# The prologue of a fused attention and SiLU kernel: key loads by slot, another order of value and query loads, the last exponentials ahead of the first product

## The chip, the cores and the metric

The kernel runs on one core of a Trainium2 chip. The time is device microseconds of one execution; the kernel before was run five times, with a median of 285.71 us (284.96 to 286.09). One more execution was taken with the hardware profiler, and all durations inside the kernel come from that one. Its own time was 285.76 us, of which 283.8 us lie between its first and its last instruction.

## The reference

Eight batches of eight heads, 576 positions and head dimension 64 go through attention over pooled keys and values: groups of eight neighbouring positions of k and v are averaged to 72, so that each head has 576 queries and 72 keys. The result, 4608 tokens of 512 features, goes through a two-layer network with SiLU.

```python
k_p = k.reshape(B, H, Sp, pool, D).mean(axis=3)          # Sp = 72, pool = 8, D = 64
v_p = v.reshape(B, H, Sp, pool, D).mean(axis=3)
scores = scale * np.matmul(q, k_p.transpose(0, 1, 3, 2))
attn = np.exp(scores - np.max(scores, axis=-1, keepdims=True))
attn = attn / (np.sum(attn, axis=-1, keepdims=True) + 1e-09)
x = np.matmul(attn, v_p)                                  # then (tokens, 512)
h = x @ w_in                                              # 512 x 2048
g = h * (1.0 / (1.0 + np.exp(-h)))
out = g @ w_out                                           # 2048 x 512
```

## The kernel before

The tokens are worked in nine stages of 512 columns (NT = 9, NTT = 512). In each stage the up-product `up` multiplies the attention result xT with w_in, 128 hidden rows at a time, ScalarE applies SiLU and writes h_T, and then the down-product multiplies with w_out and stores. Attention for the next batch is laced into the products of the stage as fillers: `spread` runs a filler after a given step (a step is one matmul of a product). The order of instructions on each engine is the order in which the program writes them; nothing reorders them (`manual_schedule`). Each engine works through its own queue in that order and waits where an operand is not ready.

PSUM has two kinds of bank: three are called "mm" and five "at". A tile asked for under a name takes a bank of that kind that must have been read by its last reader; a matmul into it waits for that reader.

Before stage 0 there is a prologue, and it alone is touched by the change. It makes attention of the first query group of batch 0, so that the first product can begin. Its pieces:

- Keys and values of batch 0 lie as 576 rows (head and pooled position) of 8 x 64 float32, cut in slots of 128 rows: four full slots and a rest of 64 rows (`load_slots`, L245). Slots 0 to 2 are in one tile, slots 3 and 4 in another. Key slots go over the queues of SP and ScalarE; values, queries and weights go over POOL's queue, which converts queries and weights to bf16 on the way.
- `slot_sums` (L263) adds the eight positions in VectorE: 512 to 256 to 128 to 64 columns a slot, for all slots of a tile in one instruction per halving.
- `select_k` (L283) sorts the summed rows by head with small matmuls against an identity matrix that POOL makes (memset and mask, L714 and L715); a copy puts the result in SBUF. `select_v` (L299) does the same for values with a shifted identity.
- `q_transpose` (L150) transposes 32 x 32 blocks of one head half and one query half on VectorE.
- `scores` (L337) makes four PSUM tiles ("at" banks) and four exponentials on ScalarE; `denominators` (L357) sums them with matmuls and takes the reciprocal with a logarithm and an exponential on ScalarE (in stage 0, for the two late parts, with a reciprocal on VectorE, 1.9 us each); `numerators` (L376) multiplies exponentials and values, and VectorE multiplies with the reciprocal into xT.
- A part is one half of the heads (the first number) and one half of the queries (the second). Parts (0, 0) and (1, 0) give the first 288 columns of xT, with which the first product starts; parts (0, 1) and (1, 1) give the next 288, and their denominators and numerators are fillers of the first up-product, at steps 1, 5, 13 and 17.
- `warm_up` (L696) are matmuls of zeros that keep TensorE busy between the pieces.

The first up-product runs 128 hidden rows (a group g, four steps) over 288 columns for g = 0 to 10, then over the remaining 224, then g = 11 to 15 over all 512. Each group writes one "mm" bank, so that the fourth group waits for the first group's SiLU. ScalarE must load another function table (L408, `moe_tables`) between the last exponential and the first SiLU.

On POOL each load waits for the landing of the load eight places before it, because eight semaphores go round. The functions that the change touches and what calls them:

Of the kernel before, what the change touches and what calls it, by code (L numbers as in the profile page):

```python
# [27 lines left out]
FP32 = mybir.dt.float32  # L28
# [8 lines left out]
def kernel(  # L37
# [9 lines left out]
    nc = tc.nc  # L47
# [6 lines left out]
    d_ff = moe_w_in.shape[1]  # L54
# [36 lines left out]
    def ps_tile(shape, dtype, tag, name):  # L91
        return psum.tile(shape, dtype, tag=tag, bufs=banks[tag], name=name)
# [4 lines left out]
    ident = shifts[:, SP : SP + 128]  # L97
    ones = singles.tile([SP, 32], BF16, name="ones")
    warm = singles.tile([128, 512], BF16, name="warm")
    w_in_sb = singles.tile([128, KF, d_ff], BF16, name="w_in_sb")  # L100
    w_out_sb = singles.tile([128, KG, d_model], BF16, name="w_out_sb")
    w_sum = singles.tile([128, 5, KQ, CQ], BF16, name="w_sum")
# [21 lines left out]
    def load_q_half(b, f):  # L124
        for a in range(2):
            es = slice(f * QF * D, (f + 1) * QF * D)
            nc.gpsimd.dma_start(out=batches[b]["q_bf"][:, a, es], in_=q_r[b][:, a, es])
# [22 lines left out]
    def q_transpose(b, a, f):  # L150
        st = batches[b]
        n = QF * D
        nc.vector.transpose(  # L153
            out=st["qT"][:, a, f * QF : (f + 1) * QF].rearrange("r i c p -> r (i c p)"),
            in_=st["q_bf"][:, a, f * n : (f + 1) * n],
        )
# [88 lines left out]
    def load_slots(eng, b, name, i0, i1, half=None):  # L245
        es = slice(0, RE) if half is None else slice(half * RE // 2, (half + 1) * RE // 2)
        src = (k if name == "k" else v)[b].rearrange("h (sp p) d -> (h sp) (p d)", p=POOL)
        src = src[:, es]
        how = dict(accum_op=ALU.add) if half else {}
        tiles = row_tiles[name]  # L250
        w = es.stop - es.start
        if i0 == SLOTS:
            eng.dma_start(
                out=tiles[1][:REST, SLOTS - SA, :w], in_=src[128 * SLOTS :], **how
            )
        else:
            j = i0 // SA
            eng.dma_start(
                out=tiles[j][:, i0 - SA * j : i1 - SA * j, :w],
                in_=src[128 * i0 : 128 * i1].rearrange("(i r) e -> r i e", r=128), **how  # L260
            )

    def slot_sums(name, j, halves=False):  # L263
        raw = row_tiles[name][j]
        dst = rows5[name][:, SA:] if j else rows5[name][:, :SA]
        w = RE // 4 if halves else RE // 2
        while w > D:
            nc.vector.tensor_add(  # L268
                out=raw[..., :w], in0=raw[..., :w], in1=raw[..., w : 2 * w]
            )  # L270
            w //= 2
        nc.vector.tensor_add(out=dst, in0=raw[..., :D], in1=raw[..., D : 2 * D])
# [26 lines left out]
    def select_v(b, a, tag="at"):  # L299
        st = batches[b]  # L300
        if a == 0:
            st["v_ps"] = ps_tile([128, H, D], FP32, tag, "v_ps")
            st["vp"] = mid.tile([SP, H, D], BF16, tag="vp", name="vp")
        for h in range(4 * a, 4 * (a + 1)):
            segs = list(segments(h))
            for j, (i, r, sp, m) in enumerate(segs):
                x = SP + r - sp
                nc.tensor.matmul(
                    st["v_ps"][:, h, :], lhsT=shifts[:, x : x + 128], rhs=v5[:, i],
                    start=(j == 0), stop=(j == len(segs) - 1),  # L310
                )
# [7 lines left out]
    def part(g, f):  # L319
        return ((g, f * QF, (f + 1) * QF),)  # L320
# [16 lines left out]
    def scores(b, segs):  # L337
        st = batches[b]
        w = width(segs)
        sc = [ps_tile([128, 512], FP32, "at", "sc_ps")[:SP, :w] for s in range(4)]  # L340
        for g, i0, i1, cs in seg_cols(segs):
            for c in range(2):
                for s in range(4):
                    rows = slice(32 * s, 32 * (s + 1))
                    nc.tensor.matmul(  # L345
                        sc[s][:, cs],
                        lhsT=kz[b % 2][rows, g, c, :],
                        rhs=st["qT"][rows, g, i0:i1, c, :],
                        start=(c == 0), stop=(c == 1),
                    )  # L350
        es = mid.tile([SP, 4, VW], BF16, tag="es", bufs=4, name="es")[:, :, :w]
        for s in range(4):
            nc.scalar.activation(es[:, s, :], sc[s], func=AF.Exp, scale=score_scale)  # L353
        st["es", segs] = es


    def denominators(b, segs, on_dve=False):  # L357
        st = batches[b]
        w = width(segs)
        es = st["es", segs]  # L360
        den_ps = ps_tile([128, 512], FP32, "at", "den_ps")
        for s in range(4):
            nc.tensor.matmul(  # L363
                den_ps[32 * s : 32 * (s + 1), :w],
                lhsT=ones, rhs=es[:, s, :], start=True, stop=True,
            )
        rec = mid.tile([128, VW], FP32, tag="rec", bufs=4, name="rec")[:, :w]
        if on_dve:
            nc.vector.reciprocal(rec, den_ps[:, :w])
        else:  # L370
            lnd = mid.tile([128, VW], FP32, tag="lnd", name="lnd")[:, :w]
            nc.scalar.activation(lnd, den_ps[:, :w], func=AF.Ln)  # L372
            nc.scalar.activation(rec, lnd, func=AF.Exp, scale=-1.0)
        st["rec", segs] = rec
# [29 lines left out]
    def attn_tables():  # L404
        nc.scalar.preload_act_table_set("natural_log_exp_and_others")
# [124 lines left out]
            pass  # L530

    def plain(t, step, g, n0, n):
        hp_ps = ps_tile([128, 512], FP32, "mm", "hp_ps")
        c0 = (t * NTT + n0) % NX

        for r0, r1 in ((0, min(n, NX - c0)), (min(n, NX - c0), n)):
            for kk in range(KF) if r1 > r0 else ():
                if r0 == 0:
                    next(step)
                x0 = (c0 + r0) % NX  # L540
                nc.tensor.matmul(  # L541
                    hp_ps[:, r0:r1],
                    lhsT=w_in_sb[:, kk, g * 128 : (g + 1) * 128],
                    rhs=xT[:, kk, x0 : x0 + r1 - r0],
                    start=(kk == 0), stop=(kk == KF - 1),
                )
        nc.scalar.activation(h_T[:, g, n0 : n0 + n], hp_ps[:, :n], func=AF.Silu)  # L547
# [148 lines left out]
    def warm_up(n):  # L696
        for _ in range(n):
            nc.tensor.matmul(warm_ps, lhsT=warm[:, :128], rhs=warm, start=True, stop=True)  # L698

    load_slots(nc.sync, 0, "k", 0, 2)  # L700
    load_slots(nc.scalar, 0, "k", 2, 3)
    load_slots(nc.scalar, 0, "k", 3, 4)
    load_slots(nc.sync, 0, "k", 4, 5)
    load_q(0, halves=True)
    load_q_half(0, 0)
    load_slots(nc.gpsimd, 0, "v", 0, 3)
    load_q_half(0, 1)
    load_slots(nc.gpsimd, 0, "v", 3, 4)
    load_slots(nc.gpsimd, 0, "v", 4, 5)
    attn_tables()  # L710
    nc.vector.memset(warm, 0.0)
    nc.vector.memset(ones, float(POOL))
    nc.vector.memset(kp, 0.0)
    nc.gpsimd.memset(shifts, 0.0)  # L714
    make_identity(nc, ident, nomemset=True)  # L715

    for n in "kv":
        nc.vector.memset(row_tiles[n][1][REST:, SLOTS - SA], 0.0)
# [1 line left out]
    def load_w_in(c0, c1):  # L720
        for g in range(2):
            nc.gpsimd.dma_start(
                out=w_in_sb[:, 2 * g : 2 * g + 2, c0:c1], in_=w_in_r[g][:, :, c0:c1]
            )
# [6 lines left out]
        load_w_in(512 * c, 512 * (c + 1))  # L731

    act_copy = nc.scalar.copy
    warm_up(19)
    slot_sums("k", 0)
    select_k(0, 0)
    copy_k(0, 0, act_copy)
    warm_up(4)
    q_transpose(0, 0, 0)
    scores(0, part(0, 0))  # L740
    slot_sums("k", 1)
# [3 lines left out]
    q_transpose(0, 1, 0)  # L745
    warm_up(2)
    scores(0, part(1, 0))
    denominators(0, part(0, 0))
    slot_sums("v", 0)
    warm_up(2)  # L750
    select_v(0, 0, "mm")
    copy_v(0, 0, act_copy)
    denominators(0, part(1, 0))
    q_transpose(0, 0, 1)
    scores(0, part(0, 1))
    slot_sums("v", 1)
    warm_up(1)
    numerators(0, part(0, 0), ("mm", "at"))
    warm_up(2)
    select_v(0, 1, "mm")  # L760
    copy_v(0, 1)
    q_transpose(0, 1, 1)
    warm_up(2)
    numerators(0, part(1, 0), ("mm", "at"))
    scores(0, part(1, 1))
    warm_up(2)
    load_slots(nc.gpsimd, 1, "k", 0, 3)
    load_slots(nc.gpsimd, 1, "k", 3, 4)
    load_slots(nc.gpsimd, 1, "k", 4, 5)
    load_q(1)  # L770
    load_w_in(1536, d_ff)
    for c in range(3):
        load_w_out(c)
    load_slots(nc.gpsimd, 1, "v", 0, 3)
# [142 lines left out]
```

The softmax here doesn't subtract the row's maximum and nothing guards it: scores larger than these inputs give would overflow.

## Time and profile before

| | |
|---|---|
| median of five runs | 285.71 us (284.96 to 286.09) |
| profiled execution, its own time | 285.76 us |
| its span, first to last instruction | 283.8 us |
| TensorE busy (matmul) | 276.4 us, 97% of the span |
| VectorE busy | 225.6 us, 79% |
| ScalarE busy | 183.8 us, 65% |
| POOL busy | 60.7 us, 21% |
| first matmul of the first up-product | 17.48 us after the start of the span |
| from then without a gap of TensorE | from 21.93 us, to 28.00 us and on |

Times inside the profile are microseconds from the first instruction. A line of a timeline gives start, length, engine, source line, operation, written and read tiles with shapes, how many instructions were merged in it, and in brackets how long the engine stood idle before it and what ended the wait. The matmul lengths contain the fill of the array, so that back-to-back matmuls start closer together than they are long. A line of the list of DMA issues gives the tiles, the queue, how many issues, their size (in the type of the destination) and the time from issue to landing.

### The profile page before, as it was taken

Reading aid. Unit: us, or ns where it says so; the run is one execution under the profiler, and the core shown is the slowest. Engines: PE = TensorE matmul, PEld = TensorE weight load, DVE = VectorE, ACT = ScalarE, POOL = GpSimd, SP = SyncE. Lnnn points to the kernel's source line nnn. Section 1 sums busy time; section 2 is a strip of 40 time slices with the busy share of each in tenths; the row PEclk is TensorE's granted clock in tenths of the full one; section 3 lists DMA queues with packets and bytes.
Section 4 is the critical chain, followed back from the end, with each engine's and each line's share of the span. In section 5 each row is a group of like instructions: output and inputs, shape, how many; then the busy total and the mean of one; then the engine's idle time right before and its main releaser. Section 6 shows DMA issues by size and latency. Waiting matters only on the chain.

```text
span 283.8 us, 6889 instructions
## 1 busy us (share of the span) xinstructions
PE 276.4 (97%) x2773; PEld 194.6 (69%) x2793; DVE 225.6 (79%) x404; ACT 183.8 (65%) x359; POOL 60.7 (21%) x78
## 2 busy tenths in 40 slices
PE   8989999999999999999999999999999999999995
PEld 3338544466777677767888786688667767787684
DVE  4887836989978898879896998799888786836773
ACT  1678676568567875687668857885779467326700
POOL 8654316342140214021402130542000000000000
PEclk9999999999999999999999999999999999999999
DMA  7999998895749763985498539597830032005003
GB/s 205 280 259 229 211 308 170 235 180 102 152 59 198 171 132 49 190 202 108 77 195 178 88 85 178 131 141 112 144 91 0 2 98 52 2 17 132 1 18 133
DMA packets 31376, 37.70 MB, mean 133 GB/s; under 512 B 10352, under 2 KB 22256, under 8 KB 31344
## 3 DMA queue, kind: packets, MB, share of 16 engines
q0 software_dynamic: 23840, 26.77, 52.1%
q1 hardware_dynamic: 6928, 9.58, 12.2%
q10 hardware_dynamic: 576, 0.92, 0.9%
q8 instruction: 22, 0.36, 0.5%
q14 instruction: 10, 0.08, 0.1%
HBM read 36.70 MB, written 9.44 MB: 163 GB/s over the span
## 4 chain that ended last, share of the span: by engine, by line
PE 93%; DVE 3%; ACT 2%; issue 1%; DVEq 0%
PE hp_ps L541 25%; PE o_psP L649 15%; PE o_psQ L649 15%; PE u_psP L482 7%; PE u_psQ L482 7%; PE o_psR L649 5%; PE sc_ps L345 4%; PE o_ps L576 3%; PE warm_ps L698 3%; PE nu_ps L389 2%; PE u_psR L482 2%; PE den_ps L363 2%; ACT es L353 1%; DVE w_sum L627 1%; DVE xT L398 1%
## 5 line engine op out<-in xcount | busy, mean ns | idle before, releaser
L541 PE MATMUL hp_ps<-xT,w_in_sb 128*128 128x512 bf16 (+3 forms) x397 | 80.1, 338 | 1.4 <-ACT h_T L547 0.4
L649 PEld LDWEIGHTS <-h_sum 128*128 128x128 bf16 x640 | 60.6, 98 | 11.9 <-issue 1.3
L547 ACT ACTIVATE h_T<-hp_ps 128x512 bf16<-128x512 f32 (+2 forms) x95 | 51.4, 546 | 25.2 <-PE hp_ps L541 24.2
L541 PEld LDWEIGHTS <-w_in_sb 128*128 128x128 bf16 x412 | 39.3, 98 | 25.0 <-issue 1.4
L609 DVE TENSOR_TENSOR h_sum<-h_T 128x1024 bf16<-128x1024 bf16 (+1 forms) x72 | 50.9, 744 | 7.0 <-ACT h_T L547 7.0
L353 ACT ACTIVATE es<-sc_ps 72x384 bf16<-72x384 f32 (+1 forms) x100 | 39.1, 470 | 10.0 <-PE sc_ps L345 10.0
L482 PEld LDWEIGHTS <-w_sum 128*128 128x128 bf16 x300 | 29.4, 98 | 7.7
L649 PEld LDWEIGHTS <-h_T 128*128 128x128 bf16 x256 | 24.1, 98 | 4.4 <-issue 0.9
L398 DVE TENSOR_TENSOR xT<-nu_ps,rec 128x384 bf16<-128x384 f32 (+1 forms) x50 | 23.9, 532 | 0.2
L372 ACT ACTIVATE lnd<-den_ps 128x384 f32<-128x384 f32 (+1 forms) x23 | 11.2, 485 | 19.3 <-PE den_ps L363 19.3
L153 DVE STREAM_TRANSPOSE qT<-q_bf 128x576 bf16<-128x576 bf16 x32 | 23.0, 755 | 0.4 <-DMA q_bf<-in_q_dram 0.4
L490 ACT ACTIVATE h_T<-c_sb 128x512 bf16<-128x512 f32 x30 | 18.1, 627 | 5.7 <-DVE c_sb L514 5.7
L268 DVE TENSOR_TENSOR raw<-raw 128x384 f32<-128x384 f32 (+3 forms) x20 | 12.3, 617 | 8.0 <-DMA raw<-in_v_dram 5.0
L177 POOL DMA_DIRECT2D raw<-in_k_dram x5 | 7.2, 1430 | 52.8 <-DMA raw<-in_k_dram 52.8
L553 POOL DMA_DIRECT2D out_dram<-o_sb x1 | 0.6, 617 | 79.7 <-issue 79.7
L649 PE MATMUL o_psP<-w_out_sb,h_sum 128*128 128x256 bf16 x128 | 17.6, 273 | 0.0
L514 DVE TENSOR_TENSOR c_sb<-u_psP,t_sb 128x512 f32<-128x512 f32 x15 | 10.3, 689 | 8.2 <-PE u_psP L482 3.6
L649 PE MATMUL o_psQ<-w_sum,h_sum 128*128 128x256 bf16 x128 | 16.7, 273 | 0.0
L649 PE MATMUL o_psQ<-w_out_sb,h_sum 128*128 128x256 bf16 x128 | 16.6, 273 | 0.0
L649 PE MATMUL o_psP<-w_sum,h_T 128*128 128x256 bf16 x128 | 16.5, 273 | 0.0
L649 PE MATMUL o_psQ<-w_sum,h_T 128*128 128x256 bf16 x128 | 16.5, 273 | 0.0
L649 PE MATMUL o_psR<-w_sum,h_sum 128*128 128x256 bf16 x128 | 15.7, 273 | 0.0
(80 smaller groups left out, 439.3 us busy)
## 6 DMA issues: line engine op xcount, KB each, us to landing
out_dram<-o_sb SPq DMA_DIRECT2D x128, 64.0 KB, 4.5
raw<-in_k_dram POOLq DMA_DIRECT2D x10, 576.0 KB, 10.0
raw<-in_v_dram POOLq DMA_DIRECT2D x10, 576.0 KB, 8.0
q_bf<-in_q_dram POOLq DMA_DIRECT2D x6, 576.0 KB, 13.6
w_in_sb<-in_moe_w_in_dram POOLq DMA_DIRECT2D x8, 256.0 KB, 8.4
w_out_sb<-in_moe_w_out_dram POOLq DMA_DIRECT2D x4, 512.0 KB, 13.9
raw<-in_v_dram POOLq DMA_DIRECT2D x2, 768.0 KB, 11.4
raw<-in_k_dram POOLq DMA_DIRECT2D x1, 768.0 KB, 10.1
```

The costliest lines, as they stand in the source:

```text
L153: nc.vector.transpose(out=st["qT"][:, a, f * QF : (f + 1) * QF].rearrange("r i c p -> r (i c p)"), in_=st["q_bf"][:, a, f * n : (f + 1) * n],)
L268: nc.vector.tensor_add(out=raw[..., :w], in0=raw[..., :w], in1=raw[..., w : 2 * w])
L345: nc.tensor.matmul(sc[s][:, cs], lhsT=kz[b % 2][rows, g, c, :], rhs=st["qT"][rows, g, i0:i1, c, :], start=(c == 0), stop=(c == 1),)
L353: nc.scalar.activation(es[:, s, :], sc[s], func=AF.Exp, scale=score_scale)
L372: nc.scalar.activation(lnd, den_ps[:, :w], func=AF.Ln)
L398: nc.vector.tensor_mul(out=xT[:, 2 * g0 + c : 2 * (g0 + ng - 1) + c + 1 : 2, cols], in0=nu[c][:, :w].rearrange("r (g n) -> r g n", g=ng), ...
L482: nc.tensor.matmul(ps[bank][:, u, :], lhsT=w[:, kk, 128 * u : 128 * (u + 1)], rhs=x[:, kk, :], start=first and u == 0 and kk == 0, stop=kk ...
L490: nc.scalar.activation(h_T[:, g : g + 2, j * NQ : (j + 1) * NQ], src, func=AF.Silu)
L541: nc.tensor.matmul(hp_ps[:, r0:r1], lhsT=w_in_sb[:, kk, g * 128 : (g + 1) * 128], rhs=xT[:, kk, x0 : x0 + r1 - r0], start=(kk == 0), stop= ...
L547: nc.scalar.activation(h_T[:, g, n0 : n0 + n], hp_ps[:, :n], func=AF.Silu)
L609: nc.vector.tensor_tensor(out=h_sum[n][:, ks, :], in0=quarter(*a, ks), in1=quarter(*b, ks), op=op)
L649: nc.tensor.matmul(ps[b][:, c, :], lhsT=left(n, kt, c), rhs=W_OUT[n][:, kt, :], start=b not in begun, stop=kt == k1 - 1, skip_group_check= ...
```

## The change

Everything but `slot_sums` (which can now work on some of a tile's slots) and one bank in `plain` is the order of the prologue:

- Key slots are loaded one by one, in turn over SP (slots 0, 2, 4) and ScalarE (slots 1, 3). Before, SP took slots 0 and 1 in one load and then slot 4, ScalarE slots 2 and 3.
- Slot 0 is summed alone, then slots 1 and 2.
- The 19 warm-up matmuls before the first selection become eight, and eight float32 matmuls of 128 columns that read key slots 0 and 2, four each, and so wait for these loads (`warm_behind`). A float32 tile of zeros is their other operand. Other warm-ups are fewer or placed anew.
- On POOL's queue the identity's memset and mask go ahead of the values, and all values ahead of the second query half.
- On VectorE the sums of the last two value slots go ahead of the second query half's transposes, and both transposes ahead of the first multiplications into xT. The second copy of values moves from VectorE to ScalarE.
- The scores of the second query half go behind the second selection of values; so their exponentials stand together at the end of the prologue on ScalarE.
- The fourth group of the first product takes an "at" bank instead of an "mm" bank.
- Of the later loads, the last quarter of w_in goes ahead of the next batch's queries.

```diff
-    def slot_sums(name, j, halves=False):
-        raw = row_tiles[name][j]
-        dst = rows5[name][:, SA:] if j else rows5[name][:, :SA]
+    def slot_sums(name, j, halves=False, part=slice(None)):
+        raw = row_tiles[name][j][:, part]
+        dst = (rows5[name][:, SA:] if j else rows5[name][:, :SA])[:, part]
...
     def plain(t, step, g, n0, n):
-        hp_ps = ps_tile([128, 512], FP32, "mm", "hp_ps")
+        tag = "at" if (t, g, n0) == (0, 3, 0) else "mm"
+        hp_ps = ps_tile([128, 512], FP32, tag, "hp_ps")
...
-    load_slots(nc.sync, 0, "k", 0, 2)
-    load_slots(nc.scalar, 0, "k", 2, 3)
-    load_slots(nc.scalar, 0, "k", 3, 4)
-    load_slots(nc.sync, 0, "k", 4, 5)
+    def warm_behind(rhs, n):
+        for _ in range(n):
+            nc.tensor.matmul(
+                warm_ps[:, : rhs.shape[-1]], lhsT=warm32, rhs=rhs, start=True, stop=True
+            )
+
+    for i in range(SLOTS + 1):
+        load_slots((nc.sync, nc.scalar)[i % 2], 0, "k", i, i + 1)
     load_q(0, halves=True)
     load_q_half(0, 0)
+    nc.gpsimd.memset(shifts, 0.0)
+    make_identity(nc, ident, nomemset=True)
     load_slots(nc.gpsimd, 0, "v", 0, 3)
-    load_q_half(0, 1)
     load_slots(nc.gpsimd, 0, "v", 3, 4)
     load_slots(nc.gpsimd, 0, "v", 4, 5)
+    load_q_half(0, 1)
     attn_tables()
     nc.vector.memset(warm, 0.0)
+    nc.vector.memset(warm32, 0.0)
...
-    nc.gpsimd.memset(shifts, 0.0)
-    make_identity(nc, ident, nomemset=True)
...
-    warm_up(19)
-    slot_sums("k", 0)
+    warm_up(8)
+    warm_behind(row_tiles["k"][0][:, 0, RE - 128 :], 4)
+    warm_behind(row_tiles["k"][0][:, SA - 1, RE - 128 :], 4)
+    slot_sums("k", 0, part=slice(0, 1))
+    slot_sums("k", 0, part=slice(1, SA))
     select_k(0, 0)
     copy_k(0, 0, act_copy)
-    warm_up(4)
+    warm_up(2)
...
+    slot_sums("v", 0)
+    warm_up(1)
     denominators(0, part(0, 0))
-    slot_sums("v", 0)
-    warm_up(2)
+    warm_up(3)
     select_v(0, 0, "mm")
     copy_v(0, 0, act_copy)
     denominators(0, part(1, 0))
+    slot_sums("v", 1)
     q_transpose(0, 0, 1)
-    scores(0, part(0, 1))
-    slot_sums("v", 1)
-    warm_up(1)
-    numerators(0, part(0, 0), ("mm", "at"))
-    warm_up(2)
-    select_v(0, 1, "mm")
-    copy_v(0, 1)
     q_transpose(0, 1, 1)
     warm_up(2)
+    numerators(0, part(0, 0), ("mm", "at"))
+    warm_up(1)
+    select_v(0, 1, "mm")
+    copy_v(0, 1, act_copy)
+    warm_up(2)
+    scores(0, part(0, 1))
     numerators(0, part(1, 0), ("mm", "at"))
+    warm_up(1)
     scores(0, part(1, 1))
-    warm_up(2)
...
+    load_w_in(1536, d_ff)
     load_q(1)
-    load_w_in(1536, d_ff)
```

More of the change, by code (lines that the diff above doesn't have):

```diff
@@ L99 @@
     warm = singles.tile([128, 512], BF16, name="warm")
+    warm32 = singles.tile([128, 128], FP32, name="warm32")
     w_in_sb = singles.tile([128, KF, d_ff], BF16, name="w_in_sb")
```

## The prediction, made before the changed kernel was run

> **What bounds the kernel now.** I read the page first, for where TensorE isn't full:
>
> ```profile
> span 283.8 us, 6889 instructions
> PE 276.4 (97%) x2773; PEld 194.6 (69%) x2793; DVE 225.6 (79%) x404; ACT 183.8 (65%) x359; POOL 60.7 (21%) x78
> PE   8989999999999999999999999999999999999995
> ```
>
> TensorE is at 9 everywhere but in the first three slices (7.1 us each) and the last. A change to the prologue is worth what it moves the moment from which TensorE streams the first product without a hole. The chain that ended last, in order of time (start, length, what), says when that is:
>
> ```profile
> 1.20 6.68 PE warm_ps L698 x19
> ...
> 16.67 0.48 PE sc_ps L345 x8
> 17.15 1.29 ACT es L353 x4
> ...
> 18.45 1.28 ACT L408
> ...
> 19.75 0.42 ACT h_T L547
> ...
> 20.21 0.41 PE hp_ps L541 x2
> 20.62 0.36 PE nu_ps L389 x8
> 20.98 0.59 PE hp_ps L541 x4
> 21.57 0.36 PE nu_ps L389 x8
> 21.93 6.07 PE hp_ps L541 x55
> ```
>
> The end is set by ScalarE: last exponentials to 18.44, table load, first silu at 19.75, and only its result frees a PSUM bank. Up to there TensorE's work is filler or waits. From 21.93 it streams (up to 28.00 without a gap), so my yardstick is this point: 18 steps of the first product done, both late numerators done. VectorE's timeline (start, length, [idle before]) shows what feeds the start:
>
> ```profile
> 5.32 1.55 DVE L268 TENSOR_TENSOR raw<-raw 128x768 f32<-128x768 f32 x2 [2.69 <-DMA raw<-in_k_dram]
> 7.66 0.78 DVE L153 STREAM_TRANSPOSE qT<-q_bf 128x576 bf16<-128x576 bf16 x1 [0.40 <-DMA q_bf<-in_q_dram]
> 8.36 1.11 DVE L268 TENSOR_TENSOR raw<-raw 128x512 f32<-128x512 f32 x2
> 10.41 1.51 DVE L268 TENSOR_TENSOR raw<-raw 128x768 f32<-128x768 f32 x2
> 13.39 1.15 DVE L268 TENSOR_TENSOR raw<-raw 128x512 f32<-128x512 f32 x2 [0.40 <-DMA raw<-in_v_dram]
> ```
>
> It waits for keys to 5.32, for queries to 7.66, and is then almost without a hole to 13. The DMA issues, asked one by one, give landings (last number, us from issue):
>
> ```profile
> q_bf<-in_q_dram POOLq DMA_DIRECT2D x1, 144.0 KB, 6.4
> raw<-in_k_dram SPq DMA_DIRECT2D x1, 512.0 KB, 4.5
> ```
>
> So the first query part, issued at 1.27, lands at 7.67, and slots 0 and 1 (issued 0.74) at 5.24.
>
> **The change, part by part.**
>
> *Keys by slot.* SP carries the same bytes in the same order (slots 0, 2, 4 for 0-1, 4), ScalarE likewise (1, 3 for 2, 3); one more issue on SP (0.44 us) has nothing behind it before the stores. So slot 0 lands earlier and slot 2 at about 5.24. Slot 0's sums (rows 128x256 0.42, 128x128 0.29, plus a smaller one) lie beside the loads. Slot 0 is done when slot 2 lands, so only two slots are left to sum: the row for two slots runs from 8.36 to 9.80, 1.44, against 1.95 for three (5.32 to 7.27). First keys at 6.76: 0.51 earlier.
>
> *Fillers ahead of them.* Warm-ups stand 0.43 apart before 6 us (12 in 5.17) and 0.22 after; the 19 hold TensorE to 7.81. Eight now end at 4.6. Eight float32 matmuls of 128 columns follow, which no row shows. Floor: small selection matmuls, 12 in 0.22, so 0.02 each; ceiling: three 128x512 warm-ups each. I take one 128x512, the row nearest in place, bank and bytes: 3.5 of them at 0.43 to 6.1, 4.5 at 0.22, end 7.1. Selection of keys then starts at 7.1, not 7.81, and the keys (6.76) don't hold it. [...]
>
> *First scores.* The copy of the keys would end at 7.7, but the query part still lands at 7.67: it stays first on POOL's queue. Its transpose ends at 8.44, scores start at 8.47 (8.99 before: two fillers fewer). [...] The trace's 6.4 decides: keys half a microsecond earlier buy nothing by themselves.
>
> *VectorE to 12.31* keeps its rows: keys 8.36 to 9.80, transpose to 10.48, values 10.41 to 12.31. On ScalarE the exponentials start at 8.94 and 10.98 (9.46 and 11.44): 0.46 earlier.
>
> *POOL's order.* The memset (0.43) and mask (0.52) now go before the first value load, which is issued at 3.5, not 2.48. It landed at 2.48 + 7.6 = 10.1 with the queue busy with queries till then; cost on landing between 0 and 1.0. I take 0, since the queue is behind and VectorE needs it at 10.41. The mask is ready at 3.5, long before 7.1. The other values (landed 4.33 + 8.4 = 12.7 and 13.3) change places with the second query half (10.6 and 11.3): 384 KB of values overtake 288 KB of queries read, and landed 2.0 behind the last of these (13.3 - 11.3), so they come at most 2.0 behind the first values: 12.1; the queries then close the group at 13.3. VectorE's hole of 0.40 at 13.39 goes: values 12.23 to 13.67, both transposes to 15.05, four products to 16.6. Later loads keep their bytes ahead.
>
> *TensorE and ScalarE, 12.36 to 18.3.* Value selection 12.36 to 12.63, denominators to 12.9, two fillers to 13.3; the value copy on ScalarE ends at 13.31; numerators 13.37 to 13.9; filler, second selection 14.1 to 14.5; its copy, now on ScalarE, 14.55 to 14.9; two fillers; scores of the second query half at 14.87, where before it was 13.05. Their exponentials start at 15.34 (before 14.47), so this step is 0.87 late. The last scores reuse those four banks: the fourth waits for the fourth exponential, 16.62, then 0.05 + 0.29 (one matmul) + 0.04 puts the last exponentials at 17.0 to 18.3 (before 17.14 to 18.44). Table load to 19.59, first silu at 19.6: 0.15 gained, no more.
>
> *The extra bank.* The fourth column group now writes an "at" bank, so TensorE no longer waits at 20.21: groups 0 to 3 and the first numerators are done at 20.2 (last exponentials 18.3, denominators to 18.6, 10 steps of 0.12, numerators 0.36). But the second numerators' second half then takes the bank of group 3 and waits for its silu: three pitches of (1.02 - 0.41)/2 = 0.30 after 19.6, plus 0.41, so 20.95; half of 0.36 follows, and the yardstick is passed at 21.2 instead of 21.86 to 21.93: 0.65 gained (0.15 ScalarE, 0.5 bank).
>
> *Behind it.* The next batch's queries go behind the last up-weights: they landed at 15.41 + 11.9 = 27.3, the weights at 29.9; swapped, queries at 29.9, so the transposes (29.57) start 0.3 later and end at 32.65; scores read them at 34.76 - 0.65. Weights come earlier than needed. The first down-weights landed at 19.78 + 12.7 = 32.5, used at 34.24; 1.1 is left. The next keys' sums end at 26.7 (landing 13.27 + 10.1), selection at 27.93 - 0.65. All cover holds for a gain up to about 1.1.
>
> Sum: 285.76 (profiled run; span 283.8 and 1.96 around it) - 0.65 = 285.1. The median of the runs, 285.71, is 0.05 lower than the profiled one, so 285.1 stands for it too.
>
> **Rivals.**
>
> *The fillers become the bound (slower).* If a float32 matmul costs two or three 128x512 pieces instead of one, TensorE is late for the selection of the keys, and the scores, exponentials and copies behind it are late with it. For it: no float32 matmul is in the trace, and each of the eight brings its weights again. [...] With two (0.86, after 6.1 0.43) the eight end at 8.8, scores start at 9.45, and each step to the silu is 0.93 later: 286.0. With three, 10.2 and 287.4. Up to 7.8 they cost nothing; it turns a loss from selection at 8.5, and one over 0.2% from about 9.0, 2.1 pieces.
>
> *Nothing moves.* The late second-half scores eat the bank's gain: a slip of 0.5 between 12.36 and 14.87 (the value loads landing at 11.0, or the copy on ScalarE behind a late denominator) goes straight through the 15.34: 285.6. For it: six operations of three engines stand in a row there. Against: 0.3 to 0.4 of slack at each load.
>
> *Queries earlier too.* With the values a microsecond behind, the first queries could land at 7.1; the two fillers and the copy then bind (7.85), everything to 12.36 moves 0.6: 284.5. Against: the queries are ahead of the values in one queue already.
>
> **How the numbers follow.** Forecast 0.50 (284.8 to 285.5), nothing moves 0.20 (285.4 to 286.0), fillers 0.18 (286.0 to 287.4), earlier queries 0.12 (284.4 to 284.8). 0.2% is 0.57 us, about what these runs can tell: faster is below 285.14, slower above 286.28. Of the forecast 0.40 is below, 0.10 within; with the queries, faster 0.52. Same: 0.10 + 0.18 + 0.03 = 0.31; slower 0.15 + 0.02 = 0.17. The range 284.4 to 286.3 leaves out the dear end of the fillers.
>
> **What would show it.** First selection at 7.1 and scores at 8.5; VectorE's query wait still ending near 7.66 and no wait at 13.4; last exponentials at 17.0 just behind the ones before; silu at 19.6; no wait of the product for a silu, but one of about 0.5 of the second numerators; the product's unbroken stretch from 21.2. Wrong if float32 matmuls hold TensorE past 8, if the first value sums start after 10.6, or if the span behind 21 us changes length.

## The result and the profile after

The changed kernel takes 285.83 us (median of 44 runs, 284.88 to 289.14); the kernel before, timed beside it, 285.35 us (78 runs, 284.88 to 286.13). The ratio is 1.0025, 95% interval 1.0015 to 1.0034: slower, by little more than the 0.2% that such a measurement can tell. The forecast was 285.1, or 0.998 as a ratio to the five runs' median of 285.71 that it started from. The profiled execution of after took 287.06 us, with a span of 284.7 us.

The median doesn't tell all. The span is listed for each run: the median span of after is 284.05, against 283.5 for 35 runs of before, and 9 of the 44 runs have a mean granted TensorE clock of 0.981 to 0.994 and spans of 284.6 to 287.4. No run of those 35 is under 0.997 or above 284.1. Most of the loss isn't in the nine: the 35 runs of after at 0.997 or more have a median of 285.77 us.

The page of after, the lines that answer to those shown of before:

```profile
span 284.7 us, 6902 instructions
PE 275.7 (97%) x2777; PEld 196.1 (69%) x2797; DVE 226.1 (79%) x407; ACT 184.5 (65%) x360; POOL 60.6 (21%) x78
PE   8799998999999999999999999999999999999995
```

Two slices lost their 9: the second, 7.1 to 14.2 us, where the prologue has a hole that it hadn't before, and the seventh, 42.7 to 49.8. TensorE's timeline of after (start, length, [idle before]) shows both holes:

```profile
4.59 2.74 PE L704 MATMUL warm_ps<-raw,warm 128*128 128x128 f32 x16
7.25 0.28 PE L291 MATMUL kz_ps<-shifts,k 128*32 128x72 bf16 x12
8.00 0.44 PE L346 MATMUL sc_ps<-qT,kz 32*72 32x288 bf16 x8
...
13.65 0.34 PE L309 MATMUL v_ps<-v,shifts 128*128 128x64 bf16 x6 [1.82 <-DVE v L273]
...
15.98 0.44 PE L346 MATMUL sc_ps<-qT,kz 32*72 32x288 bf16 x8
...
21.75 0.69 PE L390 MATMUL nu_ps<-es,vp 72*32 72x288 bf16 x8
22.37 6.14 PE L543 MATMUL hp_ps<-xT,w_in_sb 128*128 128x288 bf16 x55
...
43.89 1.03 PE L578 MATMUL o_ps<-w_out_sb,h_T 128*128 128x512 bf16 x4 [0.16 <-issue]
45.44 0.59 PE L578 MATMUL o_ps<-w_out_sb,h_T 128*128 128x512 bf16 x2 [0.52 <-DMA w_out_sb<-in_moe_w_out_dram]
```

Up to 10 us all is near the forecast (keys selected at 7.25 for 7.1) or earlier (first scores at 8.00 for 8.47). Then the selection of the values stands at 13.65 behind 1.82 us of idle TensorE. The unbroken stretch of the first product starts at 22.37, against 21.86 before and 21.2 forecast. And at 45.44, in the first down-product, TensorE waits for down-weights; before had no such wait. The rows of before for the selection, the unbroken stretch and POOL's first value load:

```profile
12.36 0.33 PE L308 MATMUL v_ps<-v,shifts 128*128 128x64 bf16 x6 [0.17 <-DVE v L272]
...
21.86 6.14 PE L541 MATMUL hp_ps<-xT,w_in_sb 128*128 128x288 bf16 x55
...
2.48 0.79 POOL L258 DMA_DIRECT2D raw<-in_v_dram  x1
```

What the first hole waited for, in VectorE's and POOL's timelines of after:

```profile
7.13 0.78 DVE L154 STREAM_TRANSPOSE qT<-q_bf 128x576 bf16<-128x576 bf16 x1 [0.24 <-DMA q_bf<-in_q_dram]
11.65 1.55 DVE L269 TENSOR_TENSOR raw<-raw 128x768 f32<-128x768 f32 x2 [1.70 <-DMA raw<-in_v_dram]
```

```profile
2.48 0.42 POOL L712 MEMSET shifts<- 128x328 bf16 x1
2.97 0.29 POOL masks.py:199 TENSOR_SCALAR_AFFINE_SELECT shifts<-shifts 128x128 bf16<-128x128 bf16 x1
3.21 1.34 POOL L259 DMA_DIRECT2D raw<-in_v_dram  x2
```

The first value load, now behind memset and mask, is issued 0.73 later than before (2.48) and its sums start 1.24 later (10.41). The load lands in sixteen parts, each with a time of its own in the trace, and the sums wait for the last. In before the parts land between 9.59 and 10.04; in after the first at 9.17 and the eighth and ninth about 9.59, earlier than before, but the last five at 10.68 to 11.63. From there ScalarE's chain keeps its forecast lengths, only late (its timeline of after):

```profile
18.14 1.30 ACT L354 ACTIVATE es<-sc_ps 72x288 bf16<-72x288 f32 x4 [0.40 <-PE sc_ps L346]
19.46 1.28 ACT L409 ACT_TABLE_LOAD   x1
20.76 1.32 ACT L549 ACTIVATE h_T<-hp_ps 128x288 bf16<-128x288 f32 x4
```

The chain of waits of after between 27 and 46 us has for the second hole:

```profile
27.89 17.51 DMA w_out_sb<-in_moe_w_out_dram
45.40 0.04 issue
45.44 0.59 PE o_ps L578 x2
```

This is the last quarter of the down-weights. Before, it was no matter; in the timeline of before and in the answer on this tile (fewest, median and most us from issue to landing) stand:

```profile
43.38 1.46 PE L576 MATMUL o_ps<-w_out_sb,h_T 128*128 128x512 bf16 x6 [0.16 <-issue]
...
L728 POOL DMA_DIRECT2D w_out_sb<-in_moe_w_out_dram x4: 742/751/770, 19.8 to 28.9; - x4
DMA to landing us min/median/max: 12.7/13.9/14.8
```

The last issue, at 28.88, landed at 28.88 + 14.8 = 43.7. Its first reader is the fifth of those six matmuls, at 43.38 + 4 x 0.216 = 44.24 (matmuls of this row start 0.216 apart). The slack before was thus 0.54 us, less than the 0.65 that was forecast as gain.

The difference of the two spans adds up from three places: the stretch starts 0.51 later (22.37 for 21.86); from there to a matmul in the next up-product, at 58.32 in before and 59.51 in after, it takes 37.14 for 36.46, 0.68 more, which is the wait for the down-weights (0.52 in the timeline, which counts from the modelled end of the matmul before); behind it 225.2 for 225.5, 0.3 less. Together 0.9, as 284.7 for 283.8.

### The profile page after: what moved, and what is told of

Its sections match the earlier page's. It is cut to its first block, busy times and chain, and to the rows that moved or that the text cites. A ratio compares the mean times of both kernels' runs of the same rounds, so it can differ in the third digit from the quotient of the medians.

```text
span 284.7 us, 6902 instructions
## 1 busy us (share of the span) xinstructions
PE 275.7 (97%) x2777; PEld 196.1 (69%) x2797; DVE 226.1 (79%) x407; ACT 184.5 (65%) x360; POOL 60.6 (21%) x78
## 4 chain that ended last, share of the span: by engine, by line
PE 80%; DMA 15%; DVE 2%; issue 1%; POOL 0%; DVEq 0%; POOLq 0%
PE hp_ps L543 20%; PE o_psP L651 15%; PE o_psQ L651 15%; PE u_psP L483 7%; PE u_psQ L483 7%; DMA w_in_sb<-in_moe_w_in_dram 7%; DMA w_out_sb<-in_moe_w_out_dram 6%; PE o_psR L651 5%; PE sc_ps L346 3%; PE u_psR L483 2%; PE nu_ps L390 2%; DMA q_bf<-in_q_dram 2%; PE den_ps L364 2%; DVE w_sum L629 1%; DVE xT L399 1%
## 5 line engine op out<-in xcount | busy, mean ns | idle before, releaser
L269 DVE TENSOR_TENSOR raw<-raw 128x256 f32<-128x256 f32 (+4 forms) x22 | 12.7, 577 | 8.4 <-DMA raw<-in_v_dram 6.2
L578 PE MATMUL o_ps<-w_out_sb,h_T 128*128 128x512 bf16 x61 | 15.2, 380 | 0.8 <-DMA w_out_sb<-in_moe_w_out_dram 0.5
```

The source lines that it names most:

```text
L269: nc.vector.tensor_add(out=raw[..., :w], in0=raw[..., :w], in1=raw[..., w : 2 * w])
L578: nc.tensor.matmul(ps, lhsT=h_T[:, g, m * 128 : (m + 1) * 128], rhs=w_out_sb[:, g, :], start=(g == 0), stop=(g == KG - 1),)
```

## Experiments

All kernels compute the full output. Spans named for a kernel are medians over its runs unless said otherwise.

**The change again.** No edit; a second profile of it.

> The changed kernel once more, to see whether its late values are its rule or one execution's. In its profile the first value load, issued at 3.21, landed at 11.63 with five of its sixteen parts 1 to 2 us behind the others, and VectorE waited for it to 11.65 (10.41 before). If that is the rule: again a wait of more than 1 us before the first value sums, and TensorE's selection of values at about 13.6. If it is chance: values at 10.0 to 10.4, selection near 12.0 (the sums of 1.9 us behind them), unbroken product from about 20.8, span near 283.1 instead of 284.7.

285.7 (284.94 to 289.11, 12 runs), ratio 1.0018, interval 0.9995 to 1.0041. In this profile the values landed at 10.55, TensorE waited 0.96 and selected them at 12.57, and the product streamed from 21.29, 0.57 earlier than before. Yet the span is 283.9, no shorter than 283.8: TensorE waits 0.80 for the down-weights, to 44.63. So the first hole varies from one execution to the next, and a prologue that is quicker than before didn't help.

**Values ahead of the mask.**

```diff
-    nc.gpsimd.memset(shifts, 0.0)
-    make_identity(nc, ident, nomemset=True)
     load_slots(nc.gpsimd, 0, "v", 0, 3)
     load_slots(nc.gpsimd, 0, "v", 3, 4)
     load_slots(nc.gpsimd, 0, "v", 4, 5)
+    nc.gpsimd.memset(shifts, 0.0)
+    make_identity(nc, ident, nomemset=True)
     load_q_half(0, 1)
```

> The changed kernel with the identity's memset and mask behind the three value loads, so that the first of these is issued at 2.48 as before. Theory of the late issue: the 0.73 us on POOL make the values late; they land at about 10.0, selection of values at about 12.0 to 12.3, about 1.3 us less than the profile of the changed kernel and 0.7 to 1.0 less than its median. Theory of the row (three value loads without queries between them make some parts of a load late): no difference, values again at 11 or later. Theory of the keys (five key loads on two queues still run when the values start): no difference either.

285.0 (284.63 to 285.42, 11 runs), ratio 0.9982 [0.9974, 0.9991]: faster than before, near the forecast of 285.1, and no run with a clock under 0.998. Its timeline, TensorE:

```profile
11.95 0.34 PE L309 MATMUL v_ps<-v,shifts 128*128 128x64 bf16 x6
...
20.92 6.14 PE L543 MATMUL hp_ps<-xT,w_in_sb 128*128 128x288 bf16 x55
...
43.95 0.59 PE L578 MATMUL o_ps<-w_out_sb,h_T 128*128 128x512 bf16 x2 [0.48 <-DMA w_out_sb<-in_moe_w_out_dram]
```

No wait for the values, and a product 0.94 earlier than before. But the down-weights take part of it back: the span of this profile is 283.2, only 0.6 less. That its time is so near to the forecast is thus partly luck: the product starts 0.28 earlier than the forecast's 21.2, and a wait that the forecast doesn't have takes it back.

**POOL's whole first order as before,** that is, value load, second query half, other values, then the mask, with everything else of the change:

```diff
     load_slots(nc.gpsimd, 0, "v", 0, 3)
+    load_q_half(0, 1)
     load_slots(nc.gpsimd, 0, "v", 3, 4)
     load_slots(nc.gpsimd, 0, "v", 4, 5)
-    load_q_half(0, 1)
+    nc.gpsimd.memset(shifts, 0.0)
+    make_identity(nc, ident, nomemset=True)
```

> The changed kernel with the whole order of POOL's queue as before (queries, values 0 to 2, second query half, values 3 and 4, then memset and mask). Theory of the late issue and theory of the row: first values at about 10.0, selection at 12.0 to 12.4; the last values come at 13.3 as before, so their sums start then, the transposes end about 1.2 later than forecast, and of the 0.65 forecast nothing or up to 0.6 in the other direction is left. Theory of the keys: first values still at 11 or later.

286.51 (285.14 to 288.9, 12 runs), ratio 1.0049 [1.0022, 1.0076]. The other values land at 13.3; VectorE's and TensorE's timelines, and the stretches by time (start and end, length, busy time of TensorE, its weight loads, VectorE, ScalarE and POOL, then the granted clock):

```profile
13.40 1.15 DVE L269 TENSOR_TENSOR raw<-raw 128x512 f32<-128x512 f32 x2 [1.40 <-DMA raw<-in_v_dram]
...
14.93 0.37 PE L309 MATMUL v_ps<-v,shifts 128*128 128x64 bf16 x4 [1.02 <-DVE v L273]
```

```profile
13.40:14.96 1.56, 0.54 (x9) 0.27 (x6) 1.49 (x4) 0.24 (x1) 1.56 (x3) 1.00 1.23 204
14.96:18.37 3.41, 2.94 (x30) 1.10 (x30) 2.79 (x6) 1.67 (x5) 1.66 (x3) 0.50 1.22 200
```

Two things follow. With the scores behind the second values, all values must come ahead of the second query half, as the change has it. And a wait of TensorE may have a second price: here, behind a wait of 1.02, the granted clock is at half for 3.41 us from 14.96. Half of the twelve runs have a clock of 0.982 to 0.994, with spans of 284.5 to 287.1.

**Key loads in pairs, as before,** with the mask ahead of the values, and then with it behind them:

```diff
-    for i in range(SLOTS + 1):
-        load_slots((nc.sync, nc.scalar)[i % 2], 0, "k", i, i + 1)
+    load_slots(nc.sync, 0, "k", 0, 2)
+    load_slots(nc.scalar, 0, "k", 2, 3)
+    load_slots(nc.scalar, 0, "k", 3, 4)
+    load_slots(nc.sync, 0, "k", 4, 5)
```

> The changed kernel with the keys loaded as before (slots 0 and 1 in one load on SP, 2 and 3 on ScalarE, 4 on SP). Theory of the keys: values land at 10.0 to 10.4 again, 1.3 us earlier than in the changed kernel's profile, and the time falls by 0.7 to 1.0. Theories of the late issue and of the row: values at 11 or later, the time as for the changed kernel within 0.3, perhaps 0.1 longer since the first keys wait for slot 1.

> The kernel of the mask behind the values with the keys loaded in pairs as before. By the prediction keys by slot buy nothing, since the queries bind: ratio 0.998 within 0.0005. By the landings seen so far (first queries at 7.64 and 7.36 with pairs, 7.11, 6.68, 6.77 and 6.95 by slot) key loads by slot end sooner and let the queries in 0.5 sooner: then 0.3 to 0.5 us are lost, ratio 0.9992 to 1.000.

286.07 (284.72 to 286.76, 12 runs), ratio 1.0009 [0.9994, 1.0025], and 285.53 (284.7 to 286.81, 12 runs), ratio 1.0005 [0.9987, 1.0022]. (The ratio isn't that of the medians: the first's runs have a mean of 285.77.) Both fall in two groups, spans of 282.9 to 283.5 and of 284.1 to 284.6. The profile of the second is of the longer group, its TensorE timeline begins:

```profile
5.31 3.75 PE L704 MATMUL warm_ps<-raw,warm 128*128 128x128 f32 x16 [0.52 <-DMA raw<-in_k_dram]
8.99 0.32 PE L291 MATMUL kz_ps<-shifts,k 128*32 128x72 bf16 x12
```

The float32 fillers wait for the pair of slots, all run at half speed, 0.43 apart (two records each), and end 1.7 later than in after. The clock comes up late in it: two warm-ups at 9.24 still stand 0.43 apart, those at 10.58 0.22, and the trace's record of full clock starts at 10.17, against 6.11 in before and 6.23 in after. In the first's profile, of the quicker group, the fillers wait longer, 0.78, but run at full clock from the start, 0.22 apart. These two profiles suggest that the groups differ by when the clock comes up; with keys by slot the fillers wait in no profile. With the values ahead of the mask, keys by slot are worth 0.5 us over the runs (285.53 in pairs, 285.0 by slot; the intervals of the ratios just overlap).

**Only POOL's order, then POOL's order and keys by slot, in the old kernel.** Everything else as in the old kernel. The first has only the edit of POOL's lines, the second both:

```diff
-    load_slots(nc.sync, 0, "k", 0, 2)
-    load_slots(nc.scalar, 0, "k", 2, 3)
-    load_slots(nc.scalar, 0, "k", 3, 4)
-    load_slots(nc.sync, 0, "k", 4, 5)
+    for i in range(SLOTS + 1):
+        load_slots((nc.sync, nc.scalar)[i % 2], 0, "k", i, i + 1)
...
+    nc.gpsimd.memset(shifts, 0.0)
+    make_identity(nc, ident, nomemset=True)
     load_slots(nc.gpsimd, 0, "v", 0, 3)
-    load_q_half(0, 1)
     load_slots(nc.gpsimd, 0, "v", 3, 4)
     load_slots(nc.gpsimd, 0, "v", 4, 5)
+    load_q_half(0, 1)
...
-    nc.gpsimd.memset(shifts, 0.0)
-    make_identity(nc, ident, nomemset=True)
```

> The kernel before with nothing but POOL's order from the change: memset and mask ahead of the values, all values ahead of the second query half. Theory of the late issue (the 0.73 us before the first value load is the cause, whatever the keys do): value landings spread as in the changed kernel, from 10.0 to 11.6, so a part of the executions is 0.5 to 1.5 us longer than before, ratio 1.001 to 1.004 and single times over 286.5. If the key loads by slot are needed for it: ratio 0.999 to 1.000, no time over 286.2.

> The kernel before with the changed POOL order and the keys by slot, nothing else. In ten profiles the first values landed at 10.55 to 11.63 in the three that had both (keys by slot, values issued at 3.1 to 3.2), and at 9.6 to 10.2 in the seven that lacked one of them. If it is these two together: first values at 10.5 or later here too, and the ratio at 1.001 or more (1.0008 with the POOL order alone). If it takes another part of the change as well: values at 10.1 and a ratio of 0.999 to 1.0005, since the queries land 0.5 sooner.

285.6 (285.1 to 287.08, 12 runs), ratio 1.0008 [0.9996, 1.0021], values landed at 10.09; and 285.96 (285.56 to 287.2, 8 runs), ratio 1.0038 [1.0022, 1.0054], values landed at 11.06, three runs with a clock of 0.992 to 0.994. In the profiles, clearly late values come only with both parts of the change: where keys go by slot and the values are issued at 3.1 or later, the first values land at 10.19 to 11.63 (six profiles); where either is missing, at 9.62 to 10.18 (eleven profiles). The two ranges touch, though, and one of the twelve runs with POOL's order alone has a clock of 0.992 and takes 287.08 us, so how often late values come may differ rather than whether they come.

**Is it the time of issue or the mask's place?** Two unused memsets go ahead of the values, the mask stays behind them.

```diff
+    for held_tile in held:
+        nc.gpsimd.memset(held_tile, 0.0)
     load_slots(nc.gpsimd, 0, "v", 0, 3)
```

> The kernel of the mask behind the values (ratio 0.9982 to before), but with two memsets of unused tiles on POOL ahead of the values, 0.4 us each, that hold their issue about as long as memset and mask did. Theory of the late issue: as the changed kernel, ratio 1.001 to 1.004, single times over 286.5, first value sums at 10.5 or later in most executions. If it is the mask instruction or what it reads and not the time: ratio 0.998, all times under 285.6.

285.32 (284.47 to 286.21, 12 runs), ratio 0.9994 [0.9983, 1.0006]. In its profile, issued at 3.10, the values land at 11.11, TensorE waits 1.67 and drops to half clock from 14.68 to 18.10. So with keys by slot the late issue alone, without the mask, can make the hole. The median, though, is nearer to the kernel with the early issue than to the change: whether the mask's place adds something is left open.

**The fourth group's bank.** Values ahead of the mask, and the bank as before.

```diff
-        tag = "at" if (t, g, n0) == (0, 3, 0) else "mm"
-        hp_ps = ps_tile([128, 512], FP32, tag, "hp_ps")
+        hp_ps = ps_tile([128, 512], FP32, "mm", "hp_ps")
```

> The kernel of the mask behind the values with the fourth group's product back in an mm bank, as before. By the prediction's step the bank is worth 0.5 us: ratio 0.9982 goes to about 1.000. If the second late numerators, which no longer wait for the fourth silu, give it all back: ratio stays at 0.998.

285.46 (284.93 to 286.25, 12 runs), ratio 1.0002 [0.9990, 1.0014], against 0.9982 with the extra bank. The wait for the first silu is back (its TensorE timeline):

```profile
19.82 0.40 PE L542 MATMUL hp_ps<-xT,w_in_sb 128*128 128x288 bf16 x2 [0.60 <-ACT h_T L548]
```

and the product streams from 21.48, 0.56 later than with the bank (20.92). But the spans of these two profiles are 283.1 and 283.2: the later product finds its down-weights there. In this pair, half a microsecond gained at 21 us was given back at 44. Over the runs it isn't all given back: the medians are 0.46 apart in time and 0.2 in span (283.4 for 283.2), and the profile without the bank is the quickest of its twelve runs.

**Filling the first wait.** The change, with six more fillers ahead of the selection of values.

```diff
-    warm_up(3)
+    warm_up(9)
     select_v(0, 0, "mm")
```

> The changed kernel with six more fillers (1.3 us) where TensorE waits for the values. Theory of the half clock: the executions of the changed kernel over 287 us (clock 0.980 to 0.994) are those where TensorE stood still for 1 us or more for the values and then ran at half clock for 3.4 us, as the profile of the held kernel shows it at 14.68; with the wait filled none is left with a clock under 0.997, and none over 286.8, while the quick executions get 0.3 to 0.9 longer. If the low clock has another cause: single executions over 287 with clock 0.98 to 0.994 as before.

285.59 (285.24 to 285.91, 11 runs), ratio 1.0008 [1.0000, 1.0017]. No run is under 0.997 in clock, and none is long. That is less than proof: in the change, its repeat and the change with halves (below) 12 of 68 runs have a low clock, and at that rate eleven runs without one come by chance about one time in eight. What is left is 0.82 of wait for the down-weights.

**Second late numerators four steps later,** with the values ahead of the mask.

```diff
-            f_up += [(17, lambda: numerators(0, part(1, 1)))]
+            f_up += [(21, lambda: numerators(0, part(1, 1)))]
```

> The kernel of the mask behind the values with the last late numerators at step 21 of the first up-product instead of 17, so that the bank of the fourth group is free when they come. At step 17 their second half waits for the fourth silu, 0.5 to 0.6 us in each profile so far. If that wait is on the path: ratio 0.9982 goes to 0.9963 to 0.9968. If TensorE then waits elsewhere for a silu: 0.998.

285.23 (284.28 to 285.94, 12 runs), ratio 0.9991 [0.9978, 1.0003]. The wait for the fourth silu is gone and the profile's span is 282.4, the shortest of its runs, but over the runs nothing can be told from the kernel without the edit.

**The down-weights.** The last quarter is loaded in two halves, one issue each, so that its first half lands earlier. This edit was put into four kernels: the one with the values ahead of the mask, the change itself, the kernel before, and the one with later numerators.

```diff
-    load_w_out(3)
+    for g0 in (12, 14):
+        nc.gpsimd.dma_start(
+            out=w_out_sb[:, g0 : g0 + 2, :], in_=w_out_r[:, g0 : g0 + 2, :]
+        )
```

> The values ahead of the mask, and the last quarter of the down-weights loaded in two halves, one issue each. Theory (the gain runs against the down-weights): with the values first, the first product streams 0.94 us earlier than before (20.92 for 21.86), but 0.48 of wait for the last down-weights at 43.95 gives two thirds of that back (span 283.2 for 283.8). The quarter spans some 2 us of the queue, so its first half lands about 1 us earlier, and the second half is needed 0.43 later than the first: the wait falls to between 0 and 0.2, and the time is 0.4 to 0.6 below that with one load, 284.4 to 284.6. Rival (something else behind 21 us takes the gain): the wait goes or moves, and the time stays 285.0. Rival (the late parts of one DMA engine hold both halves alike): the wait stays 0.4 or more, time 285.0.

> The change as it was made, with the last quarter of the down-weights loaded in two halves. Theory: its two profiles wait 0.52 and 0.80 for that quarter; with halves 0 to 0.4 remain, so that the median comes down by 0.3 to 0.6, to 285.2 to 285.5, and the runs above 286.5 remain, since the late first values are untouched. Rival (late values are all of it): 285.8 as the change.

> The kernel before, with the last quarter of the down-weights loaded in two halves. It has no wait there: the quarter landed at 43.70 and is first read at about 44.24. Theory: no change, 285.3 to 285.5. Rival (two smaller loads help or hurt by themselves, say by the one more issue of 0.75 on POOL's queue): 0.3 or more away from that on either side.

> The values ahead of the mask, the second late numerators four steps later, and the last quarter of the down-weights in two halves. Theory: its first product streams from about 20.83 and waits 0.23 at 43.12, so 0.2 to 0.4 come off: 284.8 to 285.1; no slower than the same kernel without the later numerators. Rival (the down-weights don't matter): 285.2.

| kernel | one load: time, ratio, span | two halves: time, ratio, span |
|---|---|---|
| before | 285.35, 1, 283.5 | 285.41, 0.9998 [0.9989, 1.0006], 283.5 |
| the change | 285.83, 1.0025 [1.0015, 1.0034], 284.05 | 285.21, 0.9992 [0.9984, 1.0001], 283.25 |
| values ahead of the mask | 285.0, 0.9982 [0.9974, 0.9991], 283.2 | 284.87, 0.9986 [0.9973, 0.9998], 282.95 |
| and later numerators | 285.23, 0.9991 [0.9978, 1.0003], 283.0 | 284.2, 0.9963 [0.9952, 0.9974], 282.4 |

In the kernel before, where the quarter isn't waited for, it makes no difference. In the change it takes 0.8 off the span and the loss is gone; counting only runs at 0.997 or more of the clock, the median goes from 285.77 to 285.17 (11 of 12 runs). With later numerators it takes 0.6 off the span and 1.0 off the time, more than the 0.2 to 0.4 expected, and 0.9963 is the best of all kernels here. With the values ahead of the mask alone the time doesn't tell (0.13 off the time and 0.25 off the span; 0.4 to 0.6 off the time was expected). First profile: that kernel; second: the one with later numerators, both TensorE timelines:

```profile
42.20 1.68 PE L578 MATMUL o_ps<-w_out_sb,h_T 128*128 128x512 bf16 x7
```

```profile
42.09 1.68 PE L578 MATMUL o_ps<-w_out_sb,h_T 128*128 128x512 bf16 x7
...
44.13 0.81 PE L578 MATMUL o_ps<-w_out_sb,h_T 128*128 128x512 bf16 x3 [0.18 <-DMA w_out_sb<-in_moe_w_out_dram]
```

Seven matmuls run through where they stopped after four; 0.18 is left of the wait in the second.

The profile of the change with halves happened to be its one long run: 288.93 us, clock 0.982, span 287.2. It shows what a long run is (stretches by time, columns as above):

```profile
11.50:13.20 1.70, 0.00 (x0) 0.00 (x0) 1.63 (x4) 0.72 (x2) 1.41 (x2) 1.00 1.21 198
13.20:14.90 1.70, 1.61 (x21) 0.66 (x21) 1.63 (x5) 1.18 (x3) 1.70 (x4) 0.96 1.24 205
14.90:18.30 3.40, 3.27 (x26) 1.00 (x24) 2.53 (x6) 1.59 (x5) 2.18 (x4) 0.50 1.23 204
18.30:21.70 3.40, 3.40 (x25) 1.14 (x25) 1.73 (x2) 2.59 (x6) 1.66 (x3) 0.50 1.16 316
21.70:25.00 3.30, 3.30 (x20) 1.45 (x18) 3.03 (x4) 1.48 (x5) 0.95 (x2) 0.50 1.16 241
```

The values land at 11.27, TensorE does nothing for 1.7 us, and from about 14.8 its clock is at half, for 10.24 us, well after it works again. The product streams from 25.48, 3.1 later than in the profile of after, though the wait is the same 1.82.

## Why the prediction was wrong

**Keys and fillers: right; first scores: earlier.** The float32 fillers start 0.43 apart at half clock and 0.22 at full, as taken (in after two records each, 0.21 apart before 6 us and 0.11 behind it), like the 128x512 warm-ups (0.43 before 6 us and 0.22 behind it); selection of keys at 7.25 for 7.1. The first queries, held at 7.67 in the forecast, landed at 7.11, as the third rival has it; in the profiles they land at 6.30 to 7.54 with keys by slot, at 7.02 to 7.64 in pairs. In the profile of after it bought nothing, since the values came next. With the values early, keys by slot did buy something, 0.5 in the experiment with pairs, where the prediction says that earlier keys buy nothing by themselves.

**"POOL's order ... cost on landing between 0 and 1.0. I take 0": the first step that failed.** The bound was passed in the profile of after (11.63 for 10.04) and half reached in the second (10.55). The reason given, that the queue was behind anyway, holds for the median part of the load (9.59 for 9.85), not for the last, and the sums wait for the last. Moving just this, with the values ahead of the mask, takes the ratio from 1.0025 to 0.9982. The sign that the prediction named, sums after 10.6, is in the profile of after; the nearest rival was the second, values at 11.0 and a slip straight through. Its times, 285.4 to 286.0, hold the measured 285.83 too, but partly by luck: of the 0.51 and 0.68 that the profile of after loses, it tells of the first alone.

**The chain behind the values: right in its lengths, but a term was missing.** From the selection of values on, the distances held: 7.11 to the first silu for 7.24, 8.72 to the unbroken product for 8.84. (The terms that the prediction writes out for its 21.2 add up to 21.1; from first silu to unbroken product 1.61 was measured for 1.6.) The wait of half the second numerators for the fourth silu came (they take 0.69 in after, 0.43 where they don't wait). But no term allowed for a half clock behind the wait. In the profile with halves, a long run, it held for 10.24 us, and the product streamed 3.1 later than in after behind the same wait of 1.82. For the other runs of after with a low clock there is only an estimate: 3.41 us at half go with a mean of 0.994 in the profile with POOL's whole first order as before, 10.24 with 0.982 in the one with halves, so 0.994 is about one such stretch and 0.981 about three. That the wait for the values set it off there is an inference, which the kernel with fillers supports but doesn't prove. It isn't what moved the median, since that is 285.77 without these runs.

**"The first down-weights landed at ... 32.5, used at 34.24; 1.1 is left. ... All cover holds for a gain up to about 1.1": the second step that failed,** and in both profiles of after, which ran at full clock, the one that decides. The first quarter had 1.79 of cover before the change (landed at 32.45, read at 34.24), 1.1 behind a gain of 0.65; the last had 0.54. It lands later besides: 45.40 and 44.59 in the two profiles of after for 43.70, though issued 1.0 and 0.4 earlier. With values issued at 3.1 or later the last quarter lands at 44.24 in the mean (seven profiles of one load, 43.35 to 45.40), with the earlier issue at 43.39 (six profiles, 42.83 to 43.91). They are 0.85 apart, so the 0.7 that memset and mask take at 2.48 seems to be there still at 44; the groups overlap, so this isn't shown. In both profiles of after TensorE waits for this load, and the end follows it: landing plus 239.3 gives the span of each within 0.1. So in these two profiles the first hole was not even the last limit, and the halves alone bring the change to 0.9992.

**The extra bank: right in its place and size, 0.56 for 0.5 at 21 us,** but in the pair of profiles with and without it the down-weights took it back; over the runs 0.2 to 0.46 us were left. The last exponentials right behind the earlier ones, and the values overtaking the second query half, did what was forecast: without the latter VectorE waits 1.40.

**The median as one number.** The sum stood for every execution. Before's runs lie within 1.3 us; those of after within 4.3, with landings that differ by a microsecond between two profiles.

Left open: why some of the sixteen parts fall behind when keys by slot and a later issue meet, and why the halves gained so little in the kernel with the values ahead of the mask and so much in the one with later numerators. The swap of the last up-weights and the next queries, and the moves on VectorE and ScalarE, were not run apart.

## What to carry to other kernels

Before a gain at one place is counted, look for the slack of every later load by its own landing and first reader: the last piece of a weight that comes in four pieces can have a third of the cover of the first (0.54 for 1.79 here). An instruction put ahead of a load on its queue may delay loads far behind it too (here the last down-weights landed at 44.24 for 43.39 in the mean, in groups that overlap), so put memsets and masks behind the loads where their reader allows it. Try spare matmuls in a wait of TensorE, beside shortening it: behind waits of 1.02 to 1.82 us the clock fell to half in three profiles here, and in one of them that cost more than the wait (3.1 us of delay, for a wait of 1.82 as in the profile of after). With such a wait filled none of eleven runs was long, which is less than proof.

## What the hardware showed that was not expected

- In three profiles the granted clock of TensorE dropped to half after a standstill in the prologue: for 3.41 us from 14.96 behind one of 1.02 (POOL's whole first order as before), for 3.42 from 14.68 behind one of 1.67 (the two unused memsets), and for 10.24 from 14.78 behind one of 1.82 (the change with halves). Each drop came when TensorE was at work again, 0.03, 1.55 and 1.49 us after its next matmul began. A standstill of 1.82 in the profile of after, and one of 0.96 in the second profile of it, left the clock full (1.00 in every stretch from 0 to 20 us). So the length of the standstill alone doesn't tell whether the clock falls; what does was not shown.
- In the profile of after the last of the sixteen parts of a load was 2.0 us behind the middle ones (11.63 for 9.59) and, for the last down-weights, 3.0 (45.40 for 42.37), while the middle ones were on time (9.85 and 42.16 in before). A forecast of a landing from bytes and queue alone misses this.
